# Two slices of the hidden layer in one cast and one subtraction: an attention and two-MLP kernel on one core

## The chip, the cores and the metric

The kernel runs on one core of a Trainium2 chip. The time is that of one launch on the device, in microseconds, lower is better; it is given as the median of some launches of the same program. The engines are PE (matmuls, TensorE), ACT (ScalarE), DVE (VectorE), POOL (GpSimd) and SP, which here issues the DMAs. Each engine works through its own queue of instructions in a fixed order and waits at an instruction until what it needs is there.

## The reference, cut to what matters

```
kv_pool = kv.reshape(B, H // r, r, W // r, r, C).mean(axis=(2, 4))
k = v = kv_pool.reshape(B, -1, C) @ w_sr            # 768 keys of 128
a = softmax(q @ k.T / sqrt(C));  x = a @ v          # 12288 tokens of 128
h = x @ w_in1;  g = max(h, 0) + alpha * min(h, 0)   # 2048 hidden columns
y = g @ w_out1
h = y @ w_in2;  g = h * sigmoid(1.702 * h)          # 2048 hidden columns
out = g @ w_out2
```

## The kernel before

Every float32 matmul is made of three float16 ones. An operand x is split into a high part hi = float16(x) and a low part lo = float16(x - hi), and `mm3` adds up W_hi x_hi + W_hi x_lo + W_lo x_hi in PSUM. So each slice of a hidden layer needs, between its two matmuls, the activation (one ACT and one DVE instruction), a cast to float16 for the high part (ACT), and a subtraction for the low part (POOL or DVE).

The 12288 tokens are 24 blocks of 512 columns, j = 0 to 23, and the 2048 hidden columns are 16 slices of 128, m = 0 to 15. This text writes the matmul groups as L1(j,m) (`l1`, x @ w_in1, bank tiles h), L2(j,m) (`l2`, adds to y1), L3(j,m) (`l3`, tiles h) and L4(j,m) (`l4`, adds to y2), each three matmuls of 512 columns. The loop runs over steps t = 16 j + m. One step holds L1 of block j, L2 some steps later (`L2_LAG`), L3 of a block that is 31 steps back (`L3_LAG`, so nearly two blocks), L4 another five steps back (`L4_LAG`), and a piece of the attention of a later block: scores S (`a_s`, six matmuls of 384 columns; then the maximum on DVE, exp on ACT, the normalised high part `ah` on ACT, the low part `al` on DVE, two transposing DMAs) or a sixth of a @ v (`a_v`). A block has four pieces S(j,0) to S(j,3).

Names of the instructions that the steps below speak of, by block and slice:

- relu(j,m) (ACT, L332) and mul1(j,m) (DVE, L333): activation of the first layer, from tile h to tile g1, in place. c1 (ACT, L340) and the subtraction at L341 (POOL): its high and low part.
- tanh(j,m) (ACT, L387) and mul2(j,m) (DVE, L388): the same for the second layer, h to g2; c2 (ACT, L395) and L397 (POOL, and DVE for block 0, for one slice in four, and for half of the last block).
- ql, xl, yl (DVE, L307, in `parts`): the low parts of the query block, of the attention output x and of y. qh, xh, yh (ACT, L306) are the high parts before them. ql and yl read two tiles of SBUF, xl one of PSUM and one of SBUF.
- yc (ACT, L358) and ta (DVE, L290, in `top_of`) read y1 of a finished block; ob (ACT, L412) reads y2 of a finished block.

Two pools of PSUM set the turns. `ps_h` has three banks that L1 and L3 take in turn: L1(j,m), L3(j-2,m+1), L1(j,m+1) and so on. A bank comes free when mul1 or mul2 has read it, so that each L3 waits for the mul1 of the L1 three groups earlier, and each L1 for the mul2 of such an L3. `ps_y` has two banks for y1 and y2: the first matmul of L2(j,0) waits until yc and ta have read y1 of block j-1, that of L4(j,0) until ob has read y2 of block j-1.

The program is written by steps, but the order in each engine's queue is set when it is built, by a scheduler with its own estimates; what stands in the queues is shown below.

Of the kernel before, what the change touches and what calls it, by code (L numbers as in the profile page):

```python
# [37 lines left out]
ATT_START = [-18, -5] + [KF * j - 25 for j in range(2, NB)]  # L40
ATT_S = [(0, 2, 2, 6), (0, 3, 6, 9)] + [(0, 4, 7, 12)] * (NB - 2)
# [12 lines left out]
def attn_moe_kernel(ctx: ExitStack, tc: tile.TileContext, q, kv, w_sr, w_in1, w_out1, alpha, w_in2, w_out2, out):  # L54
    nc = tc.nc
    const = ctx.enter_context(tc.tile_pool(name="const", bufs=1))
    raw_p = ctx.enter_context(tc.tile_pool(name="raw", bufs=6))
    cv_p = ctx.enter_context(tc.tile_pool(name="cv", bufs=2))
    sm_p = ctx.enter_context(tc.tile_pool(name="smp", bufs=2))
    q_p = ctx.enter_context(tc.tile_pool(name="qp", bufs=2))  # L60
    at_p = ctx.enter_context(tc.tile_pool(name="atp", bufs=2))
# [136 lines left out]
    def flush():  # L198
        while late:
            late.pop(0)()  # L200
# [115 lines left out]
        late.append(lambda: parts(xh[j], xl[j], xa, xsc[j][0]))  # L316


    g1, g2, y1, y2, yh, yl, yc, ysc = ({} for _ in range(8))
    h1, h3, gg = {}, {}, {}  # L320

    def l1(j, m):
# [2 lines left out]
        mm3(h, wh["w1"][:, ms], wl["w1"][:, ms], xh[j], xl[j], True, True)  # L325
        h1[j, m] = h

    def l1_act(j, m):
        h = h1.pop((j, m))
        g = t_p.tile([P, TB], F32, tag="g1", name="g1", bufs=3)  # L330

        nc.scalar.activation(g, h, AF.Relu, scale=-1.0)  # L332
        nc.vector.scalar_tensor_tensor(out=g, in0=g, scalar=oma[:, m:m + 1], in1=h, op0=ALU.mult, op1=ALU.add)  # L333
        gg[j, m, 1] = g

    def l1_split(j, m):
        hi = g_p.tile([P, TB], F16, tag="g1h", name="g1h")
        lo = g_p.tile([P, TB], F16, tag="g1l", name="g1l")
        g = gg.pop((j, m, 1))
# [42 lines left out]

    def l3_act(j, m):
        h = h3.pop((j, m))
        g = t_p.tile([P, TB], F32, tag="g2", name="g2", bufs=3)
# [3 lines left out]
        gg[j, m, 2] = g

    def l3_split(j, m):
        hi = g_p.tile([P, TB], F16, tag="g2h", name="g2h")
        lo = g_p.tile([P, TB], F16, tag="g2l", name="g2l")
        g = gg.pop((j, m, 2))
        nc.scalar.copy(hi, g)  # L395
# [237 lines left out]
```

## Time and profile before

| | |
|---|---|
| median of 3 launches | 1296.91 us (1295.08 to 1300.04) |
| the profiled execution | 1297.24 us, its span 1295.5 us, granted TensorE clock 0.983 on the mean |
| PE busy | 1224.9 us, 95% |
| ACT busy | 1108.0 us, 86% |
| DVE busy | 1036.3 us, 80% |
| POOL busy | 780.7 us, 60% |
| DMA | 21 GB/s of HBM traffic over the span |

The profiled execution took 1.7 us more than its span. An instruction's time in the trace goes from its start to its end, and on one engine the next can start a little before the end of the one before; so two sums are to be kept apart, that of the durations (busy) and that of the distances from start to start. Matmuls overlap most: a record of a 512-column matmul is 0.38 us long, and the next starts 0.216 us after it. Rows that read `[idle before <-releaser]` show only idle time that is longer than this overlap.

### The profile page before, as it was taken

The page shows a single profiled execution, that of the slowest core. Times are in us where ns is not written, and L with a number is a line of the kernel's source. Part 1 is how long each engine was busy: PE and PEld are TensorE (multiplying, and loading weights), DVE is VectorE, ACT ScalarE, POOL GpSimd, SP SyncE. Part 2 cuts the span into 40 slices and gives each one's busy share as a digit, 9 for nine tenths or more (in the row PEclk, how much of TensorE's full clock was granted, in tenths as well). Part 3 has the DMA queues.
Part 4 walks back from the last instruction along what each step waited for, and adds up shares of the span by engine and source line. Part 5 has one row for each costly group of instructions (what it writes and reads, how often), then busy time and mean ns, then how long its engine had stood idle before and what let it go on. Part 6 is the DMA issues. An engine that isn't in the chain of part 4 may idle for free.

```text
span 1295.5 us, 17938 instructions
## 1 busy us (share of the span) xinstructions
PE 1224.9 (95%) x5730; PEld 561.7 (43%) x5730; DVE 1036.3 (80%) x1887; ACT 1108.0 (86%) x1964; POOL 780.7 (60%) x670
## 2 busy tenths in 40 slices
PE   3467999999999999999999999999999999999998
PEld 2123444444444444444444444444444444444443
DVE  7888898778787887887887787887878878877666
ACT  1467899899898898898998998988988988988998
POOL 1045545675675666666665666756756666657774
PEclk9688999999999999999999999999999999999999
DMA  8922322121121221211121121222212212110000
GB/s 308 246 47 42 56 36 53 26 53 43 36 53 34 45 48 31 53 42 37 42 53 37 42 53 25 53 42 38 53 33 45 47 32 45 33 37 21 10 9 17
DMA packets 165375, 66.65 MB, mean 51 GB/s; under 512 B 156448, under 2 KB 156576, under 8 KB 164256
## 3 DMA queue, kind: packets, MB, share of 16 engines
q1 hardware_dynamic: 165280, 65.51, 22.4%
q8 instruction: 45, 0.74, 0.2%
q14 instruction: 50, 0.41, 0.1%
HBM read 21.05 MB, written 6.29 MB: 21 GB/s over the span
## 4 chain that ended last, share of the span: by engine, by line
PE 54%; ACT 16%; DVE 13%; issue 4%; POOLq 0%; ACTq 0%
PE h L103 8%; PE h L105 7%; PE h L104 7%; PE y L104 7%; PE y L105 7%; PE y L103 7%; ACT g L332 4%; DVE g L333 3%; ACT g L387 3%; ACT s L248 3%; ACT g1h L340 2%; DVE g L388 2%; PE xacc L103 2%; PE xacc L105 2%; PE xacc L104 2%
## 5 line engine op out<-in xcount | busy, mean ns | idle before, releaser
L341 POOL TENSOR_TENSOR g1l<-g,g1h 128x512 f16<-128x512 f32 x384 | 456.3, 1194 | 319.8 <-ACT g1h L340 315.4
L397 POOL TENSOR_TENSOR g2l<-g,g2h 128x512 f16<-128x512 f32 x272 | 314.9, 1158 | 120.7 <-ACT g2h L395 110.9
L387 ACT ACTIVATE g<-h,yu 128x512 f32<-128x512 f32 x384 | 269.0, 701 | 103.2 <-PE h L105 99.9
L388 DVE SCALAR_TENSOR_TENSOR g<-g,h 128x512 f32<-128x512 f32 x384 | 262.8, 685 | 110.2 <-ACT g L387 104.4
L333 DVE SCALAR_TENSOR_TENSOR g<-g,oma,h 128x512 f32<-128x512 f32 x384 | 285.2, 743 | 54.3 <-ACT g L332 48.5
L332 ACT ACTIVATE g<-h 128x512 f32<-128x512 f32 x384 | 235.4, 613 | 18.0 <-PE h L105 7.2
L395 ACT CAST g2h<-g 128x512 f16<-128x512 f32 x384 | 243.4, 634 | 3.3 <-PE y L105 1.2
L340 ACT CAST g1h<-g 128x512 f16<-128x512 f32 x384 | 244.0, 636 | 1.0 <-PE y L105 0.5
L104 PE MATMUL y<-g1l,w2h 128*128 128x512 f16 x384 | 146.6, 382 | 11.3 <-POOL g1l L341 11.1
L103 PE MATMUL h<-xh,w1h 128*128 128x512 f16 x384 | 145.5, 380 | 5.5 <-ACT xh L306 3.2
L103 PE MATMUL h<-yh,w3h 128*128 128x512 f16 x384 | 145.4, 379 | 3.8 <-DVE g L333 0.8
L104 PE MATMUL h<-xl,w1h 128*128 128x512 f16 x384 | 146.4, 381 | 1.6 <-DVE xl L307 0.3
L105 PE MATMUL y<-g1h,w2l 128*128 128x512 f16 x384 | 146.7, 382 | 0.0
L103 PE MATMUL y<-g1h,w2h 128*128 128x512 f16 x384 | 146.4, 381 | 0.1
L105 PE MATMUL h<-xh,w1l 128*128 128x512 f16 x384 | 146.4, 381 | 0.0
L104 PE MATMUL y<-g2l,w4h 128*128 128x512 f16 x384 | 145.7, 379 | 0.5 <-POOL g2l L397 0.5
L105 PE MATMUL y<-g2h,w4l 128*128 128x512 f16 x384 | 145.7, 379 | 0.0
L103 PE MATMUL y<-g2h,w4h 128*128 128x512 f16 x384 | 145.7, 379 | 0.0
L105 PE MATMUL h<-yh,w3l 128*128 128x512 f16 x384 | 145.5, 379 | 0.0
L104 PE MATMUL h<-yl,w3h 128*128 128x512 f16 x384 | 145.5, 379 | 0.0
L238 DVE TENSOR_REDUCE nm<-s 128x1 f32<-128x768 f32 x96 | 91.5, 953 | 12.3 <-PE s L233 8.1
L397 DVE TENSOR_TENSOR g2l<-g,g2h 128x512 f16<-128x512 f32 x112 | 90.7, 810 | 9.7 <-ACT g2h L395 9.7
(224 smaller groups left out, 1644.6 us busy)
## 6 DMA issues: line engine op xcount, KB each, us to landing
q<-in_q SPq DMA_DIRECT2D x24, 256.0 KB, 2.6
kv<-in_kv SPq DMA_DIRECT2D x12, 512.0 KB, 4.8
out<-ob SPq DMA_DIRECT2D x24, 256.0 KB, 2.0
raw_w<-in_moe_w_in SPq DMA_DIRECT2D x4, 1024.0 KB, 9.1
raw_w<-in_moe_w_out SPq DMA_DIRECT2D x4, 1024.0 KB, 6.3
eh<-ah SPq DMA_TRANSPOSE x96, 2.7
wsr<-in_w_sr SPq DMA_DIRECT2D x1, 64.0 KB, 2.2
al<-in_moe_alpha SPq DMA_DIRECT2D x1, 8.0 KB, 1.8
```

Of the source, the lines that this page charges most:

```text
L103: mm(out=o, lhsT=wh, rhs=xh, start=start, stop=False)
L104: mm(out=o, lhsT=wh, rhs=xl, start=False, stop=False)
L105: mm(out=o, lhsT=wl, rhs=xh, start=False, stop=stop)
L238: nc.vector.tensor_reduce(out=nm, in_=s[:, :, 0:HALF], axis=AX.XY, op=ALU.max, negate=True)
L332: nc.scalar.activation(g, h, AF.Relu, scale=-1.0)
L333: nc.vector.scalar_tensor_tensor(out=g, in0=g, scalar=oma[:, m:m + 1], in1=h, op0=ALU.mult, op1=ALU.add)
L340: nc.scalar.copy(hi, g)
L341: nc.gpsimd.tensor_tensor(out=lo, in0=g, in1=hi, op=ALU.subtract)
L387: nc.scalar.activation(g, h, AF.Tanh, scale=ysc[j][:, 0:1])
L388: nc.vector.scalar_tensor_tensor(out=g, in0=g, scalar=1.0, in1=h, op0=ALU.add, op1=ALU.mult)
L395: nc.scalar.copy(hi, g)
L397: e.tensor_tensor(out=lo, in0=g, in1=hi, op=ALU.subtract)
```

## The change

From the second block on (for the second layer from the first block on) two neighbouring slices, m even and m + 1, share one tile of 2 x 512 columns. The activations still write 512 columns each, into a half of the pair. At the odd slice one cast and one subtraction of 1024 columns make the high and low parts of both. All subtractions are on POOL; those that DVE had are gone from it. Since the even slice now waits for the odd one, L2 runs 6 steps behind L1 and not 4 (block 0 keeps 4), and L4 37 steps and not 36. The pairs' pool `pairs` (three buffers of each tile) lies where the raw weights were, and is opened at t = 16, when these are done with.

```diff
-L2_LAG, L3_LAG, L4_LAG = 4, 31, 36
+L2_FIRST, L2_LAG, L3_LAG, L4_LAG = 4, 6, 31, 37
...
+    def hidden(j, m, n):
+        if j == 0 and n == 1:
+            gg[j, m, n] = t_p.tile([P, TB], F32, tag="g1", name="g1", bufs=3)
+            return gg[j, m, n]
+        if m % 2 == 0:
+            gg[j, m // 2, n] = pair_p.tile([P, 2, TB], F32, tag=f"gp{n}", name=f"gp{n}")
+        return gg[j, m // 2, n][:, m % 2, :]
+
+    def split(j, m, n):
+        if j == 0 and n == 1:
+            hi, lo = (g_p.tile([P, TB], F16, tag="g1" + x, name="g1" + x) for x in "hl")
+            g = gg.pop((j, m, n))
+            gs[j, m, n] = hi, lo
+        elif m % 2:
+            hi, lo = (pair_p.tile([P, 2, TB], F16, tag=f"gp{n}{x}", name=f"gp{n}{x}") for x in "hl")
+            g = gg.pop((j, m // 2, n))
+            for i in range(2):
+                gs[j, m - 1 + i, n] = hi[:, i, :], lo[:, i, :]
+        else:
+            return
+        nc.scalar.copy(hi, g)
+        nc.gpsimd.tensor_tensor(out=lo, in0=g, in1=hi, op=ALU.subtract)
...
-        nc.scalar.copy(hi, g)
-        e = nc.vector if j == 0 or m % 4 == 3 or j == NB - 1 and m % 2 else nc.gpsimd
-        e.tensor_tensor(out=lo, in0=g, in1=hi, op=ALU.subtract)
-        g2[j, m] = hi, lo
...
-        if x := at(t, L2_LAG):
-            l2(*x)
+        for lag in (L2_FIRST, L2_LAG):
+            if (x := at(t, lag)) and (x[0] == 0) == (lag == L2_FIRST):
+                l2(*x)
...
-        for f, lag in ((x_scale, -2), (x_split, -1), (y_scale, L2_LAG + KF), (y_split, L2_LAG + KF + 2)):
-            if (x := at(t, lag)) and x[1] == 0:
-                f(x[0])
+        for f, lag in ((x_scale, -2), (x_split, -1), (y_scale, KF), (y_split, KF + 2)):
+            for j in range(NB):
+                if t == KF * j + lag + (0 if lag < 0 else L2_LAG if j else L2_FIRST):
+                    f(j)
...
+        if t == KF:
+            raw_ctx.close()
+            pair_p = ctx.enter_context(tc.tile_pool(name="pairs", bufs=3, side="right", reuse_waits="tile"))
```

The queues around the turn of a block show most of what moves. The first place is ACT where L2 goes from block 10 to block 11; before, the rows are tanh(9,3), yc(10), c1(11,2), relu(11,3), c2(9,2), ob(8), tanh(9,4), the exp of S(12,3), qh(13), c2(9,3), relu(11,4), c1(11,3).

```order
L387 ACTIVATE g2_6921<-h3_6901,yu_6393 128x512
L358 COPY yc_6911<-y1_6361 128x512
L340 CAST g1h_6973<-g1_6905 128x512
L332 ACTIVATE g1_6958<-h1_6928 128x512
L395 CAST g2h_6924<-g2_6887 128x512
L412 ACTIVATE ob_6935<-y2_6380,yu_5785 128x512
L387 ACTIVATE g2_6977<-h3_6954,yu_6393 128x512
L248 ACTIVATE s_6938,sm_6992<-s_6938,nm_6945,qu_6359 128x2x384
L306 ACTIVATE qh_6946<-q13_6344,qc_6951 128x512
L395 CAST g2h_6980<-g2_6921 128x512
L332 ACTIVATE g1_7006<-h1_6984 128x512
L340 CAST g1h_7015<-g1_6958 128x512
```

Now they are relu(11,3), the pair cast of (9,2) and (9,3), the pair cast of (11,2) and (11,3), tanh(9,4), the exp of S(12,3), qh(13), ob(8), relu(11,4), tanh(9,5), yc(10), ah(12,3), relu(11,5).

```order
L359 ACTIVATE gp1_6131<-h1_6143 128x512
L352 CAST gp2h_6186<-gp2_6113 128x1024
L352 CAST gp1h_6221<-gp1_6131 128x1024
L405 ACTIVATE gp2_6183<-h3_6166,yu_5741 128x512
L250 ACTIVATE s_6150,sm_6200<-s_6150,nm_6157,qu_5650 128x2x384
L308 ACTIVATE qh_6158<-q13_5636,qc_6163 128x512
L420 ACTIVATE ob_6197<-y2_5703,yu_5213 128x512
L359 ACTIVATE gp1_6209<-h1_6190 128x512
L405 ACTIVATE gp2_6183<-h3_6205,yu_5741 128x512
L376 COPY yc_6215<-y1_5716 128x512
L264 ACTIVATE ah_6235<-s_6150,r_6202 128x768
L359 ACTIVATE gp1_6209<-h1_6227 128x512
```

ob(8) and yc(10) stood ahead of this exp and now stand behind it, and the two casts of single slices behind it are gone; two casts of pairs stand ahead of it.

The second place is DVE at the same turn, before: mul2(9,4), two small ones for S(12,3), two for y, ql(13), the subtraction of slice (9,3), mul1(11,4), yu, mul2(9,5), al(12,3), mul1(11,5). ta(10), which reads y1_6361, stands eight rows ahead of the first of these.

```order
L388 SCALAR_TENSOR_TENSOR g2_6977<-g2_6977,h3_6954 128x512
L254 TENSOR_SCALAR r_6994<-sm_6992 128x1
L255 RECIPROCAL r_6994<-r_6994 128x1
L109 TENSOR_SCALAR yp_6999<-yt_6997 128x1
L111 TENSOR_SCALAR yc_7000<-yp_6999,kyc_108 128x1
L307 SCALAR_TENSOR_TENSOR ql_6947<-q13_6344,qc_6951,qh_6946 128x512
L397 TENSOR_TENSOR g2l_6981<-g2_6921,g2h_6980 128x512
L333 SCALAR_TENSOR_TENSOR g1_7006<-g1_7006,oma_104,h1_6984 128x512
L111 TENSOR_SCALAR yu_7001<-kk_110,yp_6999,xp_6156 128x2
L388 SCALAR_TENSOR_TENSOR g2_7019<-g2_7019,h3_7002 128x512
L273 SCALAR_TENSOR_TENSOR al__7064<-s_6938,r_6994,ah_7033 128x768
L333 SCALAR_TENSOR_TENSOR g1_7040<-g1_7040,oma_104,h1_7026 128x512
```

And now: mul2(9,4), r, its reciprocal, ql(13), mul1(11,4), mul2(9,5), ta(10), al(12,3), yd, mul1(11,5).

```order
L406 SCALAR_TENSOR_TENSOR gp2_6183<-gp2_6183,h3_6166 128x512
L256 TENSOR_SCALAR r_6202<-sm_6200 128x1
L257 RECIPROCAL r_6202<-r_6202 128x1
L309 SCALAR_TENSOR_TENSOR ql_6159<-q13_5636,qc_6163,qh_6158 128x512
L360 SCALAR_TENSOR_TENSOR gp1_6209<-gp1_6209,oma_104,h1_6190 128x512
L406 SCALAR_TENSOR_TENSOR gp2_6183<-gp2_6183,h3_6205 128x512
L292 TENSOR_REDUCE ta_6218<-y1_5716 128x1
L275 SCALAR_TENSOR_TENSOR al__6262<-s_6150,r_6202,ah_6235 128x768
L111 TENSOR_SCALAR yd_6216<-ta_6218 128x1
L360 SCALAR_TENSOR_TENSOR gp1_6209<-gp1_6209,oma_104,h1_6227 128x512
```

The subtraction is gone, and ta(10) has moved behind ql(13), mul1(11,4) and mul2(9,5).

On PE the same turn reads, in groups, before: L2(10,15), L1(11,3), L4(8,15), S(12,3), L3(9,4), L2(11,0), L1(11,4), L4(9,0), L3(9,5). Now it reads: L1(11,3), L4(8,14), S(12,3), L3(9,4), L2(10,14), L1(11,4), L4(8,15), L3(9,5), L2(10,15), L1(11,5), L4(9,0), L3(9,6), the first matmul of L1(11,6), L2(11,0), the rest of L1(11,6), L4(9,1), L3(9,7). The step after L2(10,15) has no L2.

The third place is ACT at the end of the program, where only L3 and L4 of block 23 are left. Before, tanh(23,15) is followed by the casts of slices 14 and 15.

```order
L387 ACTIVATE g2_14968<-h3_14964,yu_14602 128x512
L395 CAST g2h_14971<-g2_14954 128x512
L387 ACTIVATE g2_14982<-h3_14978,yu_14602 128x512
L395 CAST g2h_14985<-g2_14968 128x512
L395 CAST g2h_14992<-g2_14982 128x512
L412 ACTIVATE ob_15008<-y2_14834,yu_14602 128x512
```

Now the last pair's cast of 1024 columns comes behind tanh(23,15).

```order
L405 ACTIVATE gp2_13072<-h3_13082,yu_12817 128x512
L405 ACTIVATE gp2_13095<-h3_13091,yu_12817 128x512
L352 CAST gp2h_13098<-gp2_13072 128x1024
L405 ACTIVATE gp2_13095<-h3_13105,yu_12817 128x512
L352 CAST gp2h_13114<-gp2_13095 128x1024
L420 ACTIVATE ob_13133<-y2_12995,yu_12817 128x512
```

The high part of slice 14 had a cast of its own that could start before mul2(23,15); now it comes with that of slice 15.

## Rows read from the trace of the kernel before

**Rows 1.** Windows: busy time of each engine, two stretches (start, middle), then clock.

```profile
136.00:165.40 29.40, 27.25 (x130) 12.19 (x128) 24.24 (x45) 25.24 (x46) 15.47 (x13) 1.00 0.37 64
565.70:615.78 50.08, 49.86 (x239) 22.92 (x237) 40.38 (x74) 44.97 (x82) 32.34 (x29) 1.00 0.20 43
```

**Rows 2.** Timeline, PE and DVE: four places of one block, start and duration in us.

```profile
621.87 0.38 PE L105 MATMUL y<-g2h,w4l 128*128 128x512 f16 x1
622.15 0.38 PE L103 MATMUL h<-yh,w3h 128*128 128x512 f16 x1
...
624.26 0.73 DVE L333 SCALAR_TENSOR_TENSOR g<-g,oma,h 128x512 f32<-128x512 f32 x1
624.54 0.38 PE L105 MATMUL y<-g2h,w4l 128*128 128x512 f16 x1
625.05 0.38 PE L103 MATMUL h<-yh,w3h 128*128 128x512 f16 x1
...
656.70 0.38 PE L103 MATMUL y<-g2h,w4h 128*128 128x512 f16 x1
657.15 0.38 PE L104 MATMUL h<-xl,w1h 128*128 128x512 f16 x1
...
660.21 0.74 DVE L333 SCALAR_TENSOR_TENSOR g<-g,oma,h 128x512 f32<-128x512 f32 x1
660.60 0.38 PE L103 MATMUL y<-g1h,w2h 128*128 128x512 f16 x1
661.00 0.38 PE L103 MATMUL h<-yh,w3h 128*128 128x512 f16 x1
```

**Rows 3.** Timeline, ACT and PE at the turn of block 10 to 11.

```profile
615.88 0.33 PE L229 MATMUL s<-k_hi,qh 128*128 128x384 f16 x1
616.88 0.38 PE L103 MATMUL h<-yh,w3h 128*128 128x512 f16 x1
617.79 0.69 ACT L387 ACTIVATE g<-h,yu 128x512 f32<-128x512 f32 x1 [0.31 <-PE h L105]
618.37 0.96 ACT L248 ACTIVATE s<-s,nm,qu 128x768 f32<-128x768 f32 x1
619.34 0.72 ACT L306 ACTIVATE qh<-q,qc 128x512 f16<-128x512 f32 x1
619.95 0.61 ACT L395 CAST g2h<-g 128x512 f16<-128x512 f32 x1
620.46 0.60 ACT L332 ACTIVATE g<-h 128x512 f32<-128x512 f32 x1
620.95 0.62 ACT L340 CAST g1h<-g 128x512 f16<-128x512 f32 x1
```

**Rows 4.** One line's instructions (L192, L193): 1024 columns; ns, min/median/max.

```profile
L192 ACT CAST w3h<-g x2: 1046/1046/1047, 90.0 to 98.3; 128x1024 f16<-128x1024 f32 x2
L193 POOL TENSOR_TENSOR w3l<-g,w3h x2: 2127/2140/2152, 91.1 to 99.4; 128x1024 f16<-128x1024 f32 x2
```

**Rows 5.** One line's instructions (L307), and the timeline of POOL and DVE beside one.

```profile
L307 DVE SCALAR_TENSOR_TENSOR ql<-q,qc,qh x24: 736/752/753, 8.6 to 1120.9; 128x512 f16<-128x512 f32 x24
L307 DVE SCALAR_TENSOR_TENSOR yl<-yc,yh x24: 743/1129/1151, 138.1 to 1256.3; 128x512 f16<-128x512 f32 x24
...
626.12 1.16 POOL L397 TENSOR_TENSOR g2l<-g,g2h 128x512 f16<-128x512 f32 x1 [0.31 <-ACT g2h L395]
626.70 1.13 DVE L307 SCALAR_TENSOR_TENSOR yl<-yc,yh 128x512 f16<-128x512 f32 x1 [0.27 <-ACT yh L306]
```

**Rows 6.** Timeline, PE and ACT: the end of the program.

```profile
1287.60 0.38 PE L105 MATMUL h<-yh,w3l 128*128 128x512 f16 x1
1288.08 0.69 ACT L387 ACTIVATE g<-h,yu 128x512 f32<-128x512 f32 x1
...
1290.63 0.38 PE L104 MATMUL y<-g2l,w4h 128*128 128x512 f16 x1 [0.49 <-POOL g2l L397]
1291.49 0.38 PE L105 MATMUL y<-g2h,w4l 128*128 128x512 f16 x1
```

More of the change, by code (lines that the diff above doesn't have):

```diff
@@ L56, in attn_moe_kernel @@
     const = ctx.enter_context(tc.tile_pool(name="const", bufs=1))
-    raw_p = ctx.enter_context(tc.tile_pool(name="raw", bufs=6))
-    cv_p = ctx.enter_context(tc.tile_pool(name="cv", bufs=2))
+    raw_ctx = ExitStack()
+    raw_p = raw_ctx.enter_context(tc.tile_pool(name="raw", bufs=6, side="right"))
+    cv_p = raw_ctx.enter_context(tc.tile_pool(name="cv", bufs=2, side="right"))
     sm_p = ctx.enter_context(tc.tile_pool(name="smp", bufs=2))
@@ L316, in x_split @@
         late.append(lambda: parts(xh[j], xl[j], xa, xsc[j][0]))
-    g1, g2, y1, y2, yh, yl, yc, ysc = ({} for _ in range(8))
+    gs, y1, y2, yh, yl, yc, ysc = ({} for _ in range(7))
     h1, h3, gg = {}, {}, {}
@@ L326, in l1 @@
         h1[j, m] = h
+    def hidden(j, m, n):
[19 more added lines that the diff above has]
+        nc.gpsimd.tensor_tensor(out=lo, in0=g, in1=hi, op=ALU.subtract)
     def l1_act(j, m):
         h = h1.pop((j, m))
-        g = t_p.tile([P, TB], F32, tag="g1", name="g1", bufs=3)
+        g = hidden(j, m, 1)
         nc.scalar.activation(g, h, AF.Relu, scale=-1.0)
         nc.vector.scalar_tensor_tensor(out=g, in0=g, scalar=oma[:, m:m + 1], in1=h, op0=ALU.mult, op1=ALU.add)
[L334 to L339, printed above, removed]
-        nc.scalar.copy(hi, g)
-        nc.gpsimd.tensor_tensor(out=lo, in0=g, in1=hi, op=ALU.subtract)
-        g1[j, m] = hi, lo
     def l2(j, m):
@@ L346, in l2 @@
             y1[j] = ps_y.tile([P, TB], F32, tag="y", name="y1")
-        hi, lo = g1.pop((j, m))
+        hi, lo = gs.pop((j, m, 1))
         ms = slice(m * P, (m + 1) * P)
@@ L384, in l3_act @@
         h = h3.pop((j, m))
-        g = t_p.tile([P, TB], F32, tag="g2", name="g2", bufs=3)
+        g = hidden(j, m, 2)
         nc.scalar.activation(g, h, AF.Tanh, scale=ysc[j][:, 0:1])
         nc.vector.scalar_tensor_tensor(out=g, in0=g, scalar=1.0, in1=h, op0=ALU.add, op1=ALU.mult)
[L389 to L395, printed above, removed]
-        e = nc.vector if j == 0 or m % 4 == 3 or j == NB - 1 and m % 2 else nc.gpsimd
-        e.tensor_tensor(out=lo, in0=g, in1=hi, op=ALU.subtract)
-        g2[j, m] = hi, lo
     def l4(j, m):
@@ L402, in l4 @@
             y2[j] = ps_y.tile([P, TB], F32, tag="y", name="y2")
-        hi, lo = g2.pop((j, m))
+        hi, lo = gs.pop((j, m, 2))
         ms = slice(m * P, (m + 1) * P)
@@ L526, in step @@
         pieces = [(j, t - ATT_START[j]) for j in range(NB) if -8 < t - ATT_START[j] < 26]
-        if x := at(t, L2_LAG):
-            l2(*x)
+        for lag in (L2_FIRST, L2_LAG):
+            if (x := at(t, lag)) and (x[0] == 0) == (lag == L2_FIRST):
+                l2(*x)
         flush()
         if x := at(t, 2):
-            l1_split(*x)
+            split(*x, 1)
         if x := at(t, L3_LAG + 1):
@@ L534, in step @@
         if x := at(t, L3_LAG + 2):
-            l3_split(*x)
+            split(*x, 2)
         if x := at(t, 0):
```

## The prediction

> **What bounds the kernel now.** I read the busy times by windows first. In a stretch of one block in the middle PE is busy 49.86 of 50.08 us, ACT 44.97, DVE 40.38, POOL 32.34, at full granted clock [rows 1]. So PE is the bound, and work taken from ACT or DVE gains nothing by itself. What it could gain is in the waits of PE that the windows hide: a matmul is recorded 0.38 us long but starts 0.216 us after the one before (four starts from 1290.63 to 1291.49 [rows 6]), so a wait under 0.16 us shows as nothing. I therefore went through PE's starts in one block and took off 0.216 at each. Four gaps are left [rows 2]: at 622.15 (0.28 - 0.216 = 0.06; 0.07 with the third digit), at 625.05 (0.29), at 657.15 (0.23) and at 661.00 (0.18), in all 0.78 us. Three are an L3 that waits for a PSUM bank: the matmul at 625.05 starts 0.06 us after mul1(11,5), 624.26 + 0.73, has freed one; that at 661.00 starts 0.05 us after mul1(12,0), 660.21 + 0.74. The fourth, L1(12,0), waits for xl. The same four stand in each block whose turn has an exp of S(j+1,3) and a ql and which comes after the start, j = 3 to 21 (the last gap of each set in the turn to the next): 19 times, 14.8 us. That is all that the steady part holds, and 14.8 is the most that the change could gain there.
>
> **What each part costs, by rows.** A cast of 1024 columns is 1.046 us, a POOL subtraction of 1024 is 2.14 (2.13 the lowest) [rows 4]; the weights' preparation uses the same forms. Two single casts take 0.51 each from start to start (619.95 to 620.46 [rows 3]); the long one, with the same overlap of 0.10 (0.61 - 0.51), 0.945. So a pair saves ACT 0.075 us, sixteen pairs 1.2 us a block, not the 3.4 that the durations suggest. DVE loses four subtractions a block. POOL gets 16 x 2.13 = 34.1 us of 50: it keeps up. The fewer instructions are worth nothing while PE is the bound; what counts is where the rearranged queues make PE wait. I walk through the one place where its slack was used up, the turn of a block.
>
> **The turn, before and now.** Zero is the start of L3(9,4), at 616.88; S(12,3) started 1.00 earlier [rows 3]. PE now runs (0.647 a group): L3(9,4) 0, L2(10,14) 0.65, L1(11,4) 1.29, L4(8,15) 1.94, L3(9,5) 2.59, L2(10,15) 3.24, L1(11,5) 3.88, L4(9,0) 4.53, L3(9,6) 5.18, one matmul of L1(11,6) 5.82, L2(11,0) 6.04.
>
> ACT: an activation starts 0.48 after the last matmul's start (1287.60 to 1288.08 [rows 6]). L1(11,3) now starts its last matmul at -1.00 - 0.65 - 0.22 = -1.87, so relu(11,3) starts at -1.39, pair cast (9,2) at -0.90 (0.49 a relu, 620.46 to 620.95 [rows 3]), pair cast (11,2) at 0.06 (mul1(11,3) ends by then), tanh(9,4) at 1.00, exp at 1.58 (0.58 later, as before), qh at 2.55 (0.97), ob at 3.16 (0.61), relu(11,4) at 3.74, tanh(9,5) 4.23, yc 4.81. qh ends at 2.55 + 0.72 = 3.27: ql(13) is ready at 3.30.
>
> POOL: the first pair's subtraction starts 0.08 after its cast, -0.90 + 1.05 + 0.08 = 0.23, ends at 2.35; the second follows at 2.30 and ends at 4.43. So at 3.30 POOL has 1.13 us to go.
>
> What a DVE instruction with two SBUF inputs does beside POOL shows in yl: free it takes 0.743, as a rule 1.129 [rows 5]; it starts at 626.70, when POOL's subtraction (626.12 + 1.16) has 0.58 to go, and loses 0.38: the rest less 0.20. ql has the same form and has never met POOL (752 ns at the median, 753 at most [rows 5]). Now it does, and loses 1.13 - 0.20 = 0.93. mul1(11,4) behind it starts at 3.30 + 0.67 + 0.93 = 4.90 and ends at 5.64; L3(9,6) starts at 5.69 and not 5.18: **0.51**. mul2(9,5) then runs from 5.56, ta(10) from 6.16 to 6.84; L2(11,0), whose bank ta frees, could start at 6.55 by now and starts at 6.89: **0.34**. Behind them L3(9,7) finds mul1(11,5) done. The old waits at 622.15 and 625.05 are replaced by these two.
>
> The wait for xl (0.23) stays: the same S(13,2), exp, relu, xh, xl stand in the same order and at the same distance. The one at 661.00 goes: the DVE subtraction ahead of mul1(12,0) is gone, and so is a cast of 0.51 between ah and relu(12,0); mul1 would end some 0.6 earlier against 0.18 needed.
>
> Per block then 0.51 + 0.34 + 0.23 = 1.08 against 0.78, **+0.30**, times 19 = **+5.7 us**. Bounds: if ql loses nothing, mul1(11,4) waits for relu(11,4) only (ends 5.13), L3(9,6) is in time, ta still ends late by 0.32: 0.55 a block, -4.4. If ta too were in time, 0.23 a block, -10.5.
>
> The Trainium skill ("SBUF — State Buffer", section "Who interferes with whom") says that DVE with two SBUF inputs and a GpSimd instruction that reads SBUF exclude each other, and that the later one is blocked until the other has finished. yl agrees that it waits, but loses 0.20 less than the rest of POOL's instruction. By the rule to the letter ql would lose 1.13 and the sum be 0.2 a block, 3.8 us, higher.
>
> **The end.** Now the last pair ends: tanh(23,15) 0.48 after the last L3 matmul (T), 0.69 of tanh, 0.69 of mul2 and a little between: cast at T + 1.98, 1.05, POOL at T + 3.15, 2.13, and W_hi x_lo of slice 14 at T + 5.33; four matmul starts later, T + 6.19, the last one starts. With L4 one step later T comes 0.65 earlier. Before, the last one starts at 1291.49 - 1287.60 = T + 3.89 [rows 6]. So +6.19 - 0.65 - 3.89 = **+1.65**. The earlier pairs of the tail meet PE with some 0.2 us to spare or short; 0 to +0.8, taken as 0.
>
> **The start.** The queues are the same up to t = 16. From 136 to 165.4 PE is idle for 29.40 - 27.25 = 2.15 us even by the records [rows 1]. Two steps without an L2 and one without an L4 take 3 x 0.65 = 1.9 us of matmuls out of a stretch that ACT and DVE set, to be done later: 0 to +1.9. Against that the sixteen DVE subtractions of block 0 go, which can give back at most about the waits there: 0 to -1.5. I take +0.5. The pairs' pool takes the raw weights' place at t = 16, after their last use at t = 15: nothing, or one subtraction of 2.14.
>
> **Sum**, on the profiled execution's 1297.24 (0.3 over the median): 1297.2 + 5.7 + 1.65 + 0.5 = **1305.1 us**, half a per cent up and a little more (median 1296.91; 0.5% is 6.5 us, about what a measurement here can tell from no change).
>
> **Rivals.** First, what I forecast: the turn's waits grow; 1301 to 1309, since ql may lose 0.2 more (all that POOL has to go) or 0.2 less, 3.8 us over 19 turns. For it: POOL's subtraction is twice as long and stands where ql stands, and L2's bank now changes hands in 2.15 us of PE work, where before a whole S lay between. The upper end is also what the page's rule would give. 0.50.
>
> Second, no change: ql finds POOL free, since the second subtraction ends 1.1 us earlier or qh comes that much later, and the new wait for ta stands against the two old ones: 1297.2 - 4.4 + 2.2 = 1295; anything between it and the first case is here too. Against it: the casts are tied to relu(11,3), which is tied to PE. 0.27.
>
> Third, faster: shorter queues on ACT take away the bank waits and ta is in time, so that only xl's wait is left: 1297.2 - 10.5 + 2.2 = 1289. It decides when ta ends by 6.0 and not 6.84, that is if the exp of S(12,3) came 0.8 us earlier; but exp hangs on S and on tanh(9,4), both PE's, which speaks against it. 0.12.
>
> Fourth, worse: yl and yu, next on DVE, meet the longer subtractions too (up to 2.13 - 0.20 = 1.9 us instead of yl's 0.38), delay max and exp of S(13,0) by over a microsecond, and one more bank wait of 0.3 a block comes up: 1305 + 5.7 = 1311. Against it: the steps there carry attention and have some 2 us of slack by the same kind of walk. 0.11.
>
> **Chances and range.** Faster by over 0.5% (below 1290.4): the third case, 0.12. Slower (above 1303.4): the fourth and four fifths of the first, 0.51. Same: the rest, 0.37. The range, 1291 to 1312, leaves out most of the third case and the top of the fourth, some 0.18. The first case alone is 1301 to 1309.
>
> **What would show it.** Right: a block takes 50.38 us where it took 50.08; ql takes about 1.7 us, with POOL's 1024-column subtraction running; L3(9,6) starts 0.05 us after mul1(11,4), L2(11,0) 0.05 us after ta(10); the gap at xl stays 0.23, that at L3(10,2) is gone; POOL subtractions of 2.13, casts of 1.05 with 0.945 from start to start; at the end the last five matmuls follow POOL's last instruction. Wrong: ql at 0.75 us (second case), no gap at L2(11,0) (third), gaps in the steps with S(13,0) (fourth), or a start that loses or gains more than 2 us up to block 3.

## The result, and the profile after

The changed kernel takes **1305.72 us** (median of 6 launches, 1303.35 to 1308.22), the kernel before, on the same chip, 1296.41 (6 launches): a ratio of **1.0063**, 95% interval 1.0051 to 1.0076. It is slower by a little more than half a per cent. The profiled execution took 1306.35 us with a span of 1304.5.

The windows of after, the start and one block in the middle, beside [rows 1] (columns as there):

```profile
136.00:164.90 28.90, 26.95 (x131) 12.27 (x130) 23.01 (x42) 24.36 (x38) 15.35 (x8) 1.00 0.39 65
564.80:615.12 50.32, 49.79 (x238) 22.93 (x237) 39.15 (x70) 43.64 (x65) 34.23 (x17) 1.00 0.23 43
```

All three helpers of PE changed as meant: per block ACT has 1.3 us less to do, DVE 1.2 less, POOL 1.9 more, and no engine is near its limit but PE. Still the block became 0.24 us longer. As in [rows 1] the busy time of PE doesn't tell why; the turn does. The timeline of after at the turn of block 10 to 11, the place of [rows 3]:

```profile
616.55 1.05 ACT L352 CAST gp1h<-gp 128x1024 f16<-128x1024 f32 x1
616.79 2.13 POOL L353 TENSOR_TENSOR gp2l<-gp,gp2h 128x1024 f16<-128x1024 f32 x1 [0.28 <-PE qt L297]
618.88 2.13 POOL L353 TENSOR_TENSOR gp1l<-gp,gp1h 128x1024 f16<-128x1024 f32 x1
619.05 0.72 ACT L308 ACTIVATE qh<-q,qc 128x512 f16<-128x512 f32 x1
...
619.80 1.75 DVE L309 SCALAR_TENSOR_TENSOR ql<-q,qc,qh 128x512 f16<-128x512 f32 x1 [0.26 <-ACT qh L308]
621.48 0.73 DVE L360 SCALAR_TENSOR_TENSOR gp<-gp,oma,h 128x512 f32<-128x512 f32 x1
621.54 0.38 PE L107 MATMUL y<-gp2h,w4l 128*128 128x512 f16 x1
622.27 0.38 PE L105 MATMUL h<-yh,w3h 128*128 128x512 f16 x1 [0.35 <-DVE gp L360]
622.74 0.68 DVE L292 TENSOR_REDUCE ta<-y 128x1 f32<-128x512 f32 x1
622.91 0.38 PE L105 MATMUL h<-xh,w1h 128*128 128x512 f16 x1
623.47 0.38 PE L105 MATMUL y<-gp1h,w2h 128*128 128x512 f16 x1 [0.17 <-DVE ta L292]
```

ql(13) starts at 619.80, when POOL's subtraction (618.88 + 2.13 = 621.01) has 1.21 us to go, and takes 1.75 instead of 0.75. mul1(11,4) behind it ends at 622.21; L3(9,6) starts 0.06 later, 0.73 after the matmul before it where 0.216 is the pace: a wait of **0.51**. ta(10) ends at 623.42; L2(11,0) starts 0.05 later, 0.56 after the matmul before: **0.34**. The third wait, for xl, is 0.17. In all 1.03 us a block, the same in each from 3 to 21, against 0.78 [rows 2]; the wait at L3(10,2) is gone.

The same forms over the whole program (one line's instructions, ns, min/median/max), beside [rows 4, 5]:

```profile
L309 DVE SCALAR_TENSOR_TENSOR ql<-q,qc,qh x24: 729/1748/1753, 8.3 to 1123.0; 128x512 f16<-128x512 f32 x24
L309 DVE SCALAR_TENSOR_TENSOR xl<-xacc,xc,xh x24: 741/746/751, 74.4 to 1205.5; 128x512 f16<-128x512 f32 x24
L309 DVE SCALAR_TENSOR_TENSOR yl<-yc,yh x24: 740/2105/2592, 138.4 to 1263.3; 128x512 f16<-128x512 f32 x24
...
L406 DVE SCALAR_TENSOR_TENSOR gp<-gp,h x384: 670/686/690, 157.8 to 1295.7; 128x512 f32<-128x512 f32 x192
...
L352 ACT CAST gp1h<-gp x184: 1032/1046/1130, 129.4 to 1249.0; 128x1024 f16<-128x1024 f32 x184
...
L353 POOL TENSOR_TENSOR gp1l<-gp,gp1h x184: 2118/2131/2270, 130.5 to 1250.7; 128x1024 f16<-128x1024 f32 x184
```

ql and yl read two tiles of SBUF, and both now take 1.0 us longer at the median. xl stays at 0.746, but in the steady part no POOL subtraction runs beside it, so it tells nothing here. mul2 (L406) does: it has one input in PSUM, most of its 384 stand beside a POOL subtraction, and none takes more than 0.69.

The end of after (timeline), beside [rows 6]:

```profile
1294.23 0.38 PE L107 MATMUL h<-yh,w3l 128*128 128x512 f16 x1
...
1295.74 0.38 PE L105 MATMUL y<-gp2h,w4h 128*128 128x512 f16 x1
1296.37 1.04 ACT L352 CAST gp2h<-gp 128x1024 f16<-128x1024 f32 x1 [0.75 <-DVE gp L406]
1297.34 0.38 PE L106 MATMUL y<-gp2l,w4h 128*128 128x512 f16 x1 [1.22 <-POOL gp2l L353]
1297.55 2.12 POOL L353 TENSOR_TENSOR gp2l<-gp,gp2h 128x1024 f16<-128x1024 f32 x1 [0.26 <-POOL gp2l L353]
...
1298.42 0.38 PE L105 MATMUL y<-gp2h,w4h 128*128 128x512 f16 x1
1299.72 0.38 PE L106 MATMUL y<-gp2l,w4h 128*128 128x512 f16 x1 [0.93 <-POOL gp2l L353]
...
1300.58 0.38 PE L107 MATMUL y<-gp2h,w4l 128*128 128x512 f16 x1
```

The last two pairs cost 1.39 (1297.34 - 1295.74 - 0.216) and 1.09 us. Further up in the last block stand two waits that the prediction did not have:

```profile
1260.60 2.13 POOL L353 TENSOR_TENSOR gp2l<-gp,gp2h 128x1024 f16<-128x1024 f32 x1 [1.76 <-PE yt L297]
1260.93 1.82 DVE L113 TENSOR_SCALAR yu<-kk,yp,xp 128x2 f32<-128x2 f32 x1
1262.67 0.68 DVE L406 SCALAR_TENSOR_TENSOR gp<-gp,h 128x512 f32<-128x512 f32 x1
1262.77 0.38 PE L107 MATMUL y<-gp2h,w4l 128*128 128x512 f16 x1
1263.40 0.38 PE L105 MATMUL h<-yh,w3h 128*128 128x512 f16 x1 [0.24 <-DVE gp L406]
...
1264.64 1.04 ACT L352 CAST gp2h<-gp 128x1024 f16<-128x1024 f32 x1 [1.35 <-DVE gp L406]
1265.81 2.13 POOL L353 TENSOR_TENSOR gp2l<-gp,gp2h 128x1024 f16<-128x1024 f32 x1 [3.08 <-ACT gp2h L352]
...
1266.63 0.38 PE L105 MATMUL y<-gp2h,w4h 128*128 128x512 f16 x1
1267.99 0.38 PE L106 MATMUL y<-gp2l,w4h 128*128 128x512 f16 x1 [0.98 <-POOL gp2l L353]
```

yu, an instruction of two elements, stays on DVE for 1.82 us, until POOL's subtraction is over. mul2 behind it is late, so L3 waits 0.41 at 1263.40, the next pair's cast and subtraction are late too, and L4 waits 1.15 at 1267.99.

**Where the 9.1 us went.** The last matmul starts at 1300.58 in after and at 1291.49 before. I split the distance at relu(3,3) and relu(22,3), which stand at 212.59 and 1168.60 after, at 215.09 and 1166.70 before. The 19 blocks between them: 956.01 against 951.61, **+4.4**. The start: -2.50, but three groups of matmuls (3 x 0.647 = 1.94) are still owed there, because L2 and L4 stand later, so **-0.56**. From relu(22,3) on: 131.98 against 124.79, +7.19, less the 1.94 that was owed: **+5.2**.

The start is the least certain of the three, since single executions differ there. In the first 125 us, where the queues are nearly all the same, the granted TensorE clock is 0.80 in after, 0.82 before and 0.84 in e5 below (1.00 from 125 to 216 us in all three), and relu(1,0) stands at 126.91, 126.08 and 124.61. From relu(1,0) to relu(3,3), at full clock, after takes 85.68 us and before 89.01: 3.33 less, and 1.39 less when the 1.94 owed is taken off.

### The profile page after: what moved, and what is told of

It reads as the page before. It is cut to its first block, busy times and chain, and to the rows that moved or that the text cites. A ratio compares the mean times of both kernels' runs of the same rounds, so it can differ in the third digit from the quotient of the medians.

```text
span 1304.5 us, 16843 instructions
## 1 busy us (share of the span) xinstructions
PE 1225.8 (94%) x5730; PEld 562.7 (43%) x5730; DVE 992.8 (76%) x1775; ACT 1071.7 (82%) x1588; POOL 843.4 (65%) x406
## 4 chain that ended last, share of the span: by engine, by line
PE 74%; DVE 9%; ACT 3%; issue 1%; POOLq 0%; ACTq 0%
PE y L105 11%; PE y L106 11%; PE y L107 11%; PE h L106 10%; PE h L107 10%; PE h L105 10%; DVE ql L309 3%; PE xacc L106 2%; PE xacc L105 2%; PE xacc L107 2%; PE s L231 2%; PE s L232 2%; PE s L235 2%; ACT s L250 2%; DVE nm L240 1%; DVE gp L406 1%
## 5 line engine op out<-in xcount | busy, mean ns | idle before, releaser
L353 POOL TENSOR_TENSOR gp2l<-gp,gp2h 128x1024 f16<-128x1024 f32 x192 | 417.8, 2176 | 335.4 <-ACT gp2h L352 309.3
L353 POOL TENSOR_TENSOR gp1l<-gp,gp1h 128x1024 f16<-128x1024 f32 x184 | 392.4, 2133 | 33.4 <-ACT gp1h L352 20.0
L406 DVE SCALAR_TENSOR_TENSOR gp<-gp,h 128x512 f32<-128x512 f32 x384 | 262.1, 683 | 140.7 <-ACT gp L405 134.8
L360 DVE SCALAR_TENSOR_TENSOR gp<-gp,oma,h 128x512 f32<-128x512 f32 x368 | 272.9, 742 | 68.8 <-ACT gp L359 60.3
L405 ACT ACTIVATE gp<-h,yu 128x512 f32<-128x512 f32 x384 | 265.5, 692 | 53.0 <-PE h L107 50.6
L359 ACT ACTIVATE gp<-h 128x512 f32<-128x512 f32 x368 | 221.8, 604 | 53.2 <-PE h L107 52.8
L352 ACT CAST gp2h<-gp 128x1024 f16<-128x1024 f32 x192 | 200.3, 1043 | 23.8 <-DVE gp L406 23.8
L352 ACT CAST gp1h<-gp 128x1024 f16<-128x1024 f32 x184 | 192.8, 1048 | 28.8 <-DVE gp L360 28.8
L106 PE MATMUL y<-gp2l,w4h 128*128 128x512 f16 x384 | 145.5, 379 | 3.4 <-POOL gp2l L353 3.4
L105 PE MATMUL y<-gp2h,w4h 128*128 128x512 f16 x384 | 145.5, 379 | 0.0
```

The lines of the kernel that those rows point to most:

```text
L105: mm(out=o, lhsT=wh, rhs=xh, start=start, stop=False)
L106: mm(out=o, lhsT=wh, rhs=xl, start=False, stop=False)
```

## The experiments

All are made from the changed kernel unless it says otherwise. Theory A: the 1024-column subtraction keeps DVE's two-input instructions waiting, and the last pairs end late. The rivals: the lags (B), the long cast (C), ta's place. A cast or subtraction that is "halved" is two instructions of 512 columns, on the two halves of the pair's tile. A block is (relu(22,3) - relu(3,3)) / 19, and "end" is the sum of PE's waits from relu(22,3) on (distances between starts less the pace, as in the prediction). Each ratio is to the kernel before on the same chip, measured beside it.

| kernel | median us | ratio, 95% interval | block us | waits a block us | ql ns, median | end us |
|---|---|---|---|---|---|---|
| before | 1296.41 | | 50.08 | 0.78 | 752 | 0.82 |
| after | 1305.72 | 1.0063 (1.0051 to 1.0076) | 50.32 | 1.03 | 1748 | 5.74 |
| e1 lags only | 1298.43 | 1.0009 (0.9999 to 1.0018) | 50.19 | 0.88 | 752 | 0.89 |
| e2 one subtraction halved | 1296.54 | 0.9994 (0.9984 to 1.0004) | 49.85 | 0.53 | 773 | 5.73 |
| e3 ta from the copy | 1303.84 | 1.0051 (1.0039 to 1.0062) | 50.20 | 0.90 | 1745 | 5.76 |
| e4 tail by single slices | 1302.28 | 1.0043 (1.0026 to 1.0060) | 50.32 | 1.03 | 1746 | 2.67 |
| e5 another one halved | 1307.11 | 1.0071 (1.0055 to 1.0088) | 50.32 | 1.03 | 1748 | 5.71 |
| e6 all subtractions halved | 1289.52 | 0.9942 (0.9925 to 0.9959) | 49.73 | 0.43 | 860 | 2.42 |
| e7 e2 + e3 + e4 | 1294.71 | 0.9973 (0.9962 to 0.9984) | 49.85 | 0.54 | 773 | 2.69 |
| e8 e6 + e3 + e4 | 1286.32 | 0.9909 (0.9893 to 0.9925) | 49.62 | 0.32 | 859 | 0.09 |
| e9 all casts halved | 1296.58 | 0.9994 (0.9980 to 1.0007) | 50.01 | 0.72 | 1365 | 2.41 |
| e10 e6 + e9 | 1288.12 | 0.9923 (0.9901 to 0.9945) | 49.71 | 0.41 | 956 | 0.98 |
| e11 before, all on POOL | 1297.70 | 0.9997 (0.9984 to 1.0010) | 50.14 | 0.84 | 752 | 1.22 |
| e12 e10 + e3 + e4 | 1284.46 | 0.9898 (0.9878 to 0.9918) | 49.60 | 0.30 | 953 | 0.13 |

### The lags alone

In the kernel before, only the lags become 6 and 37 (with more buffers for the parts that now live longer).

```diff
-L2_LAG, L3_LAG, L4_LAG = 4, 31, 36
+L2_FIRST, L2_LAG, L3_LAG, L4_LAG = 4, 6, 31, 37
...
-        hi = g_p.tile([P, TB], F16, tag="g1h", name="g1h")
+        hi = g_p.tile([P, TB], F16, tag="g1h", name="g1h", bufs=6)
```

> The kernel before with the longer lags alone (6 and 37), each slice still cast and subtracted by itself. Theory A (the longer POOL subtraction holds up ql, and the turn of y1's bank has no scores in it): the wait at L2(j,0) for ta is there (0.3 us a turn), ql meets a 512-column subtraction at most and loses under 0.4, so a turn waits 0.5 to 0.85 us in all against 0.78 before; nothing is lost at the end: 1293 to 1299 us. Rival B (the longer lags alone cost the time, whatever the length of the instructions): 1303 to 1307 us, as the changed kernel.

No measurable change. Waits at L3(j-2,6) (0.39) and L2(j,0) (0.12) are there already; in after they are 0.51 and 0.34. But the first has another cause here. ql takes 0.75, and before mul1(j,4) behind it DVE stands idle for relu(j,4) on ACT (timeline, turn of block 10 to 11):

```profile
619.95 0.75 DVE L333 SCALAR_TENSOR_TENSOR g<-g,oma,h 128x512 f32<-128x512 f32 x1 [0.31 <-ACT g L332]
```

So the lags alone bring up a wait of this size, by ACT's queue; that in after it is ql, the next experiments show. At the turn to block 22, where no ql stands any more, L2 waits 0.67.

### One subtraction in two halves

The subtraction of slices (j,2) and (j,3), the one beside ql, becomes two POOL instructions of 512 columns. The rest stays, the cast of 1024 too.

```diff
+        if j and n == 1 and m == 3:
+            for i in range(2):
+                nc.gpsimd.tensor_tensor(out=lo[:, i, :], in0=g[:, i, :], in1=hi[:, i, :], op=ALU.subtract)
+            return
```

> The changed kernel, but the subtraction of one pair in a block, slices 2 and 3 of the first layer, in two POOL instructions of 512 columns (for blocks 1 to 23). Casts, lags, ACT's and DVE's queues stay. Theory A: ql finds the first half nearly done and takes 0.75 to 0.85 us, not 1.75; the wait at L3(j-2,6) goes from 0.51 to under 0.1, that for ta stays 0.3; 0.5 a turn less, 19 turns: about 1296 us. Rival B (lags) and rival C (the long casts on ACT ahead of the exp): the wait stays, 1305 us.

The timeline at the same turn:

```profile
615.31 2.72 POOL L355 TENSOR_TENSOR gp1l<-gp,gp1h 128x512 f16<-128x512 f32 x2
...
616.24 0.77 DVE L309 SCALAR_TENSOR_TENSOR ql<-q,qc,qh 128x512 f16<-128x512 f32 x1 [0.26 <-ACT qh L308]
617.31 0.75 DVE L364 SCALAR_TENSOR_TENSOR gp<-gp,oma,h 128x512 f32<-128x512 f32 x1 [0.29 <-ACT gp L363]
```

The same work on POOL (the row holds both halves, and they take longer than the 2.13 of one), but ql comes at the seam of the two and takes 0.77. mul1(j,4) then waits for ACT and not for ql, the wait of 0.51 is gone, that of 0.34 is 0.26, a small one of 0.10 at L1(j,11) is new, and the time is that of the kernel before: its interval holds 1. The 0.53 a block that are left come close to the 0.55 that the prediction gave for a ql that loses nothing, though the parts differ. One POOL instruction of the sixteen in a block carries more than the whole loss of the steady part (19 x 0.47 = 8.9 us against 4.4), and the end is as it was.

**The control**: the same edit with `m == 11`, whose subtraction stands far from ql.

> The changed kernel, with another pair's POOL subtraction in two halves: slices 10 and 11 of the first layer, which ql does not meet. Theory A (it is the subtraction beside ql that counts): ql stays at 1.75 us, the wait at L3(j-2,6) at 0.51; 1304 to 1307 us. Rival (shorter POOL instructions anywhere free PE): several us less.

Nothing in the turn moves, ql stays at 1748, and the time (1307.11) is no better than that of the changed kernel. So it is not shorter POOL instructions in general; what counts is what runs beside ql.

### ta from the copy

```diff
-                top_of(y, d)
+                top_of(yc[j], d)
```

ta reads the SBUF copy, so that y1's bank is free after yc.

> The changed kernel, but ta, the maximum over y, reads the copy yc in SBUF and not y1 in PSUM, so that y1's bank is free once ACT has copied it. Theory A: the wait of 0.34 us at L2(j,0) is gone, the rest stays: 0.34 x 20 = 6.8 us less, about 1299 us. Rival (PE waits there for L1(j,6)'s bank or for yc, ta only happens to end then): under 0.1 a turn less, 1304 to 1306 us.

The wait of 0.34 goes, but only 0.12 a block is gained. The next matmul that needs DVE waits instead (timeline):

```profile
621.54 1.00 DVE L275 SCALAR_TENSOR_TENSOR al__6262<-s,r,ah 128x768 f16<-128x768 f32 x1
...
622.53 0.73 DVE L360 SCALAR_TENSOR_TENSOR gp<-gp,oma,h 128x512 f32<-128x512 f32 x1
...
623.31 0.38 PE L105 MATMUL h<-yh,w3h 128*128 128x512 f16 x1
```

mul1(11,5) stands behind ql, mul1, mul2, ta and al, and comes 0.22 too late for L3(9,7). DVE's queue is late as a whole, and the edit only moves the place where PE meets it. The expected size was wrong by that.

### The tail by single slices

In the last block the second layer's slices are cast and subtracted one by one, odd ones on DVE; the lags stay.

```diff
-    h1, h3, gg = {}, {}, {}
+    h1, h3, gg, last = {}, {}, {}, {}
...
+        elif j == NB - 1 and n == 2:
+            if m % 2 == 0:
+                last[0] = [pair_p.tile([P, 2, TB], F16, tag=f"gp2{x}", name=f"gp2{x}") for x in "hl"]
+            hi, lo = (x[:, m % 2, :] for x in last[0])
+            g = gg[j, m // 2, n][:, m % 2, :]
+            gs[j, m, n] = hi, lo
+            nc.scalar.copy(hi, g)
+            (nc.vector if m % 2 else nc.gpsimd).tensor_tensor(out=lo, in0=g, in1=hi, op=ALU.subtract)
+            return
```

> The changed kernel, but the second layer of the last block casts and subtracts each slice by itself, even slices on POOL, odd ones on DVE; lags stay. Theory A: the end's waits for low parts of pairs (about 3.5 us over the last 40 us) go, 3 to 4 us less, about 1302 us. Rival (the end waits for the long lag, one step more of L4 alone): nothing less, 1305 us.

As expected. The waits behind yu (0.41 and 1.15) stay, which the pair of block 22 causes; the 3.1 us of the late pairs go.

### Everything halved, and together

All subtractions of pairs in two POOL instructions (the condition of the second experiment becomes `if j or n == 2`):

> The changed kernel, every pair's subtraction in two POOL instructions of 512 columns, casts still of 1024. Theory A: at the turns what the one halved pair gave (waits 0.53 a turn, 49.83 us a block), and at the end the low part of an even slice comes 1.0 us earlier, so that most of the 2.5 us at the last two pairs goes; 1293 to 1295 us. Rival (the end waits for the casts of pairs and the lag): 1296 to 1297 us.

The three single edits together:

> The changed kernel with three edits: the subtraction of slices 2 and 3 of the first layer in two halves, ta from the copy, the last block's second layer by single slices. Theory A: the wait at L3(j-2,6) gone as with the first edit, that at L2(j,0) gone, but most of it back at L3(j-2,7), since mul1(j,5) stands behind ta and al on DVE (0.22 of 0.34 came back with the second edit alone); the end 3.1 us shorter: 49.7 us a block, 1290 to 1293 us, some 0.3 to 0.5% below the kernel before. Rival (the edits' gains are the same wait counted twice): 1293 to 1296 us.

All subtractions halved, with the tail and ta:

> As the run with three edits, but with every pair's subtraction in two halves. Theory A: the same turns, and at the start of block 23's second layer (1.15 and 0.4 us, beside yl) something back too: 1289 to 1292 us. Rival (POOL's two instructions take 2.2 us a pair and fall behind): 1293 us or more.

The first came out 4.5 us better than theory A's middle. Besides the turn (0.43 a block, the small one of 0.10 that the second experiment had left is gone as well), the waits behind yu go, and half of those at the turn to block 22: 0.92 + 4.82 becomes 0.47 + 1.95, and relu(3,3) stands 1.1 us earlier. I had priced the place at ql alone, but other instructions of DVE gain too: yl's median falls from 2105 to 1130 ns. The three single edits together came out in the range of the rival (1293 to 1296), not of theory A: they gained less than their sum, for the reason of ta's experiment. With the one subtraction halved, taking ta's 0.26 away brings up 0.15 at L3(j-2,7) and two of 0.10, so that the block stays at 49.85. With all subtractions halved ta's edit is worth 0.11 a block (49.73 to 49.62), and the time of that run, 1286.32, lies below theory A's range.

### The casts halved

The cast in two ACT instructions, the subtraction still one of 1024 columns; then both in halves.

```diff
-        nc.scalar.copy(hi, g)
+        if j or n == 2:
+            for i in range(2):
+                nc.scalar.copy(hi[:, i, :], g[:, i, :])
+        else:
+            nc.scalar.copy(hi, g)
```

> Every pair's cast in two ACT instructions of 512 columns; the subtraction stays one POOL instruction of 1024. Theory A (the length of POOL's instruction beside ql is what costs, the long cast is not): ql still takes about 1.75 us, L3(j-2,6) still waits about 0.5 in each turn, the block stays within 50.2 to 50.5, the end still waits some 4 to 5 us: 1302 to 1308 us, as the changed kernel. Rival C (the cast of 1024 columns holds ACT too long, 0.945 us at a time, and its activations come late): the wait at L3(j-2,6) shrinks below 0.3 though ql is as long as before, 1300 us or less.

> Every pair's cast and subtraction in two instructions of 512 columns each (cast, subtraction, cast, subtraction), so that no instruction of 1024 columns is left; pairs' tiles, lags and all subtractions on POOL stay. Theory A: the time of the run with all subtractions halved (1289.5), 1287 to 1292 us, since the long cast's 0.075 us a pair lie on ACT, which PE does not wait for; block 49.6 to 49.8. Rival C: below 1286, a block of 49.5 or less. A second rival (the long cast does save something, since ACT is the next engine that PE waits for): 1294 or more.

Here theory A missed, by 5.4 us at its nearest bound: the halved casts alone bring the time of before back, with POOL's instruction as long as ever. The time and the wait are those that rival C gave; what C did not have is that ql gets shorter too. The timeline says how:

```profile
612.46 0.63 ACT L354 CAST gp2h<-gp 128x512 f16<-128x512 f32 x1
613.23 2.13 POOL L357 TENSOR_TENSOR gp2l<-gp,gp2h 128x1024 f16<-128x1024 f32 x1 [0.50 <-ACT gp2h L354]
615.31 2.13 POOL L357 TENSOR_TENSOR gp1l<-gp,gp1h 128x1024 f16<-128x1024 f32 x1
616.63 1.36 DVE L309 SCALAR_TENSOR_TENSOR ql<-q,qc,qh 128x512 f16<-128x512 f32 x1 [0.26 <-ACT qh L308]
```

The even slice is cast earlier, so that only a cast of 0.63 stands between relu(11,3) (at 611.97) and POOL: POOL starts 1.26 after that relu and not 1.66 (616.79 - 615.13 in after), 0.40 earlier. ql begins at the same place behind qh, has 0.81 of POOL ahead (617.44 - 616.63) and not 1.21, and takes 0.38 less. The wait at L3(j-2,6) falls from 0.51 to 0.11. So the mechanism of A holds to 0.02 us, but the long cast has a part in it: it sets when POOL starts. This turn gives 5.8 us over the 19 blocks (50.32 to 50.01); another 3.3 come back at the end, from relu(22,3) on (131.98 to 128.69), where the waits fall from 5.74 to 2.41. With both in halves the time is that of the halved subtractions, as A expects; the difference of 1.4 us lies within the intervals.

### All on POOL, without pairs and lags

In the kernel before, one line:

```diff
-        e = nc.vector if j == 0 or m % 4 == 3 or j == NB - 1 and m % 2 else nc.gpsimd
-        e.tensor_tensor(out=lo, in0=g, in1=hi, op=ALU.subtract)
+        nc.gpsimd.tensor_tensor(out=lo, in0=g, in1=hi, op=ALU.subtract)
```

> The kernel before, with single slices and the old lags; only the second layer's subtractions that DVE had (block 0, one slice in four, half of the last block) move to POOL, one line. Theory A (what gains is that DVE is relieved and no instruction is longer than 512 columns; the longer lags do nothing by themselves): the waits at 0.07, 0.29 and 0.18 of a turn go at least in part, a block takes 49.6 to 49.9 us, and the end no more than 1 us longer than before: 1286 to 1293 us. Rival (the longer lags are needed for it, since the low parts on POOL alone come later than L4 wants them): 1295 us or more, with waits at W_hi x_lo of L4.

No change, and neither side as stated: the time is the rival's, but in the blocks L4 does not wait for low parts. The old waits of 0.29 and 0.18 go, and that of 0.07 at L3(j-2,6) becomes 0.60 (timeline):

```profile
617.99 1.21 POOL L396 TENSOR_TENSOR g2l<-g,g2h 128x512 f16<-128x512 f32 x1 [2.09 <-ACT g2h L395]
...
618.10 1.12 DVE L111 TENSOR_SCALAR yu<-kk,yp,xp 128x2 f32<-128x2 f32 x1
619.14 0.73 DVE L333 SCALAR_TENSOR_TENSOR g<-g,oma,h 128x512 f32<-128x512 f32 x1
...
619.92 0.38 PE L103 MATMUL h<-yh,w3h 128*128 128x512 f16 x1 [0.44 <-DVE g L333]
```

The subtraction taken from DVE now runs on POOL beside yu, and DVE stands still for it all the same. In after, with the longer lags, yu comes later (626.54), at a place where PE doesn't wait for it. That the lags are needed to have it there is read from these rows; no run has all subtractions on POOL with the lags and without pairs.

### The best version

Pairs' tiles, lags and all subtractions on POOL, no instruction of 1024 columns, the tail by single slices, ta from the copy:

> Casts and subtractions of every pair in halves, the last block's second layer by single slices (odd ones' subtractions on DVE), and ta read from the copy of y1. Theory A: the 0.56 us of waits at the end and the 0.23 at ta go, a block takes 49.6, 1284 to 1287 us, the same as the run with long casts that had these three (1286.3). Rival C (long casts cost something in themselves): below 1284 us.

1284.46 us, ratio 0.9898: the fastest of all, by the ratios 1.0 per cent below the kernel before and 1.6 below the changed one (0.9898 / 1.0063). Of a block's waits 0.30 are left, and at the end 0.13. Whether it beats the run with long casts (0.9909) the intervals leave open.

## Why the prediction was right, and where its terms were not

**The outcome** was as forecast: slower, 1305.7 for 1305.1. The direction came from the mechanism; that the size came out within about a microsecond is luck. All three terms were off, the turn by -1.3 us, the end by +3.6 and the start by -1.1, and they nearly cancel.

**The turn.** The mechanism was as predicted and is shown by three runs: ql meets POOL (e2 takes most of the meeting away and e9 shortens it, and the wait follows; e5 halves elsewhere, and nothing follows). Rest 1.21 (forecast 1.13), loss 1.00 (0.93), L3(j-2,6) waits 0.51 (0.51), L2(j,0) 0.34 (0.34), L3(10,2) nothing. xl's wait is 0.17 for 0.23, which was taken over from before. With it a block takes 50.32 for 50.38, and the term is +4.4 where +5.7 stood: over by 1.3.

**The Trainium skill's rule** ("SBUF — State Buffer", section "Who interferes with whom"): DVE with two SBUF inputs and a GpSimd instruction that reads SBUF exclude each other. To the letter ql would lose all of the 1.21 us; the trace has 1.00, so the sum went by the row and not by the rule. The trace agrees on who is affected: mul2, with one input in PSUM, kept its 0.69 beside POOL's subtractions.

**The end** is the term that was mis-sized: +5.2 for +1.65. The last pair itself was right (last start at T + 6.35, forecast 6.19). Wrong were "the earlier pairs of the tail ... 0 to +0.8, taken as 0", which came to 2.35 us of waits against 0.16 before, and the turn to block 22, the last but one, which was not costed, with 0.92. Of these 2.35, 1.56 follow yu beside POOL (0.41 + 1.15), and of the 0.92, 0.45 follows yl, which takes 2.04 us there. That is the fourth rival's mechanism. It was held against it that the steps there have slack, and in blocks 3 to 21 this is so: yl takes 2.1 us and PE doesn't wait. Behind the last scores (S(23,3) at 1169) it is so only in part: yu takes 1.53 at 1225.43 and PE doesn't wait, 1.82 at 1260.93 and it does. That the missing scores are the reason is argued, not shown. Some 0.3 of the term I could not place.

**The start** was taken at +0.5 and came to -0.56, within its bounds; at full clock alone it is -1.39, close to the lower one of -1.5.

**The rivals.** "Same" fell since POOL was not free at ql. What "faster" wanted, ta in time, did not suffice when it was tried (e3): mul1(j,5) comes up behind it. With ta's edit and no subtraction longer than 512 columns (e8, e12) a block comes to 49.6 us.

## What to carry to other kernels

When work is taken from one engine and given to another, ask not only whether the other keeps up, but what runs beside its instructions and must wait for them to end: a longer instruction saves overhead where it stands and lengthens the longest wait of its neighbours. Look for the one instruction that PE's next bank depends on, and find out what starts just before it; here one subtraction of sixteen, halved, was worth 8.9 us, about as much as the whole change cost. What feeds that neighbour counts as well: with the casts halved POOL started 0.4 us earlier, and the wait at the turn all but went. The tail and the last turns are priced by a walk of their own, since slack that holds in the steady part can be gone there.

## What was not expected of the hardware

- **An instruction of two elements waits like one of 512.** yu (128 x 2, its operands in SBUF) takes 1.82 us in after beside a POOL subtraction with 1.80 to go; one-element instructions in the same place (nm, yc) keep 0.21. It was to be seen in the kernel before, where yu takes 0.28 alone and, as a rule, 0.81 beside a shorter subtraction:

```profile
L111 DVE TENSOR_SCALAR yu<-kk,yp,xp x24: 283/808/1006, 134.3 to 1255.4; 128x2 f32<-128x2 f32 x24
```

The Trainium skill ("SBUF — State Buffer", section "Who interferes with whom") says that tensor_scalar can, under conditions on its operands, enter a mode that takes the port shared with GpSimd; yu agrees. No run shows which condition the one-element ones fail.
- **A waiting DVE instruction goes before POOL's next one.** In the changed kernel, in the timeline after the same turn:

```profile
627.02 2.13 POOL L353 TENSOR_TENSOR gp1l<-gp,gp1h 128x1024 f16<-128x1024 f32 x1
627.60 2.10 DVE L309 SCALAR_TENSOR_TENSOR yl<-yc,yh 128x512 f16<-128x512 f32 x1
629.11 2.58 POOL L353 TENSOR_TENSOR gp2l<-gp,gp2h 128x1024 f16<-128x1024 f32 x1
```

yl ends at 629.70, 0.55 after POOL's first instruction; POOL's second takes 0.45 longer than 2.13. So the meeting costs both, and a seam between two POOL instructions is where a DVE instruction that is already waiting gets in. One that comes just at the seam may not: in e1 yu starts 0.02 us ahead of POOL's next subtraction, while mul1 before it on DVE is still ending, and stays until that subtraction is over.

```profile
624.91 0.75 DVE L333 SCALAR_TENSOR_TENSOR g<-g,oma,h 128x512 f32<-128x512 f32 x1
625.58 1.20 DVE L111 TENSOR_SCALAR yu<-kk,yp,xp 128x2 f32<-128x2 f32 x1
625.60 1.16 POOL L341 TENSOR_TENSOR g1l<-g,g1h 128x512 f16<-128x512 f32 x1
```
